# Channel attention on one core: 18 tiles of 64 rows in four slots, and a counted loop on TensorE

## Chip, cores, metric

One core of a Trainium2 chip, the other cores idle. The metric is the device time of one launch in microseconds. Times before and after the change are medians of fast runs; a profile is one run out of them.

## The reference

```
x: (1, 384, 384, 384) bf16, normal * 0.05;  w1d: (1,) bf16
g = mean of x over the 384*384 pixels            # one number for each channel
s = sigmoid(g * w1d[0])
out = x * s                                      # broadcast over the pixels
```

The input is 113.25 MB and so is the output. The mean is needed before the first product is right, and the ring of slots on the chip holds 264 of x's 1152 rows (256 after the change). Both kernels therefore guess: they take the sigmoid of the mean of the first rows, multiply and store with it, sum all rows meanwhile, and compare at the end. In bf16 both sigmoids are the same here, so the second pass, which is in the program for the other case, never runs.

## The kernel before

The 147,456 pixels are 1152 "rows" of 128 partitions. A tile of n rows is one DMA in which each partition moves n x 384 elements that lie on end in device memory. TensorE sums a tile by matmuls with a matrix of ones into three banks, VectorE multiplies it in place, ScalarE's queue stores it. A small planner records operations with what they read and write, and puts in the semaphore waits.

```python
WIDE = 512
EDGE, SLOT, BOTH = 44, 44, 4       # rows of the first tile, of a slot; tiles loaded on two queues
...
    def dram(view, r0, n):
        return view[r0 * P : (r0 + n) * P, :].rearrange("(p t) c -> p (t c)", p=P)
...
    def put(place, n, r0, to):
        plan.op("vector", gate(to, place, n, s_early),
                reads=["s_early"] + rows(place, n), writes=rows(to, n))
        plan.final.append(
            plan.dma("scalar", dram(o_rows, r0, n), at(to, n), reads=rows(to, n)))
...
    for k in range(BOTH):                     # halves of the first tiles on both queues
        load(places[k], sizes[k], starts[k], ("sync", "scalar"))
        if k == 0:
            plan.dma("scalar", w_one[0:1, 0:1], w1d.unsqueeze(0), writes=["w_one"])
    weight()
    add_rows(places[0], sizes[0], 0, True, True)
    add_banks(0, copy=True)
    plan.op("scalar", ...sigmoid -> s_early...)
    for k in range(1, len(sizes)):
        if k >= n_slots:                      # six slots of 44 rows
            j = k - n_slots
            put(places[j], sizes[j], starts[j], places[j])
        if k >= BOTH:
            load(places[k], sizes[k], starts[k])          # sync queue alone
        add_rows(places[k], sizes[k], 1, k == 1, k == last)
    for k in range(len(sizes) - n_slots, last):
        put(places[k], sizes[k], starts[k], places[k])
    put(places[last], sizes[last], starts[last], places[last + 1 - n_slots])
```

Of the kernel before, what the change touches and what calls it, by code (L numbers as in the profile page):

```python
# [13 lines left out]
class Planner:  # L14
# [9 lines left out]
    def __init__(self, nc, name, n_dma_sems):  # L24
        self.nc = nc
        self.streams = {e: [] for e in ("sync", "scalar", "vector", "tensor", "gpsimd")}
        self.sems = {e: nc.alloc_semaphore(f"{name}_{e}") for e in self.COMPUTE}
        self.count = {e: 0 for e in self.COMPUTE}
        self.pool = [nc.alloc_semaphore(f"{name}_dma_{i}") for i in range(n_dma_sems)]
        self.pool_uses = [0] * n_dma_sems  # L30
        self.n_dma = 0
        self.writer = {}
        self.readers = {}
        self.seen = {e: {} for e in self.streams}
        self.final = []

    def _wait(self, engine, token):
        sem, value = token
        if self.seen[engine].get(sem.name, 0) >= value:
            return  # L40
        self.seen[engine][sem.name] = value
        self.streams[engine].append(("wait", sem, value))

    def _needs(self, reads, writes):
        need = {}
        tokens = []
        for r in reads:
            if r in self.writer:
                tokens.append(self.writer[r])
        for r in writes:  # L50
            if r in self.writer:
                tokens.append(self.writer[r])
            tokens.extend(self.readers.get(r, ()))
        for sem, value in tokens:
            if need.get(sem.name, (None, 0))[1] < value:
                need[sem.name] = (sem, value)
        return list(need.values())

    def _record(self, token, reads, writes):
        for r in reads:  # L60
# [5 lines left out]
    def op(self, engine, emit, reads=(), writes=(), signal=True):  # L66


        reads, writes = list(reads), list(writes)
        for token in self._needs(reads, writes):  # L70
            if engine == "tensor" and token[0].name == self.sems["tensor"].name:
                continue
            self._wait(engine, token)
        token = (self.sems[engine], self.count[engine] + 1)
        if signal:
            self.count[engine] += 1
        self.streams[engine].append(("op", emit, self.sems[engine] if signal else None, 1))
        self._record(token, reads, writes)

    def dma(self, engine, out, in_, reads=(), writes=()):  # L80
        reads, writes = list(reads), list(writes)
        for token in self._needs(reads, writes):
            self._wait(engine, token)
        i = self.n_dma % len(self.pool)
        self.n_dma += 1
        if self.pool_uses[i]:
            self._wait(engine, (self.pool[i], 16 * self.pool_uses[i]))
        self.pool_uses[i] += 1
        token = (self.pool[i], 16 * self.pool_uses[i])
        self.streams[engine].append(  # L90
            ("op", lambda e: e.dma_start(out, in_), self.pool[i], 16)  # L91
        )
        self._record(token, reads, writes)
        return token

    def emit(self, name, e):
        for kind, a, b, *c in self.streams[name]:
            if kind == "wait":
                e.wait_ge(a, b)
            else:  # L100
                ins = a(e)
                if b is not None:
                    ins.then_inc(b, c[0])


def split(n, most):
    k = -(-n // most)
    return [n // k + (i < n % k) for i in range(k)]


WIDE = 512
EDGE, SLOT, BOTH = 44, 44, 4


def bass_standalone__channel_attn_eca__vision_kernel(
# [30 lines left out]
    def at(r0, n):  # L146
        assert r0 + n <= n_arena
        return arena[:, r0 * C : (r0 + n) * C]

    def rows(r0, n):  # L150
        return [("sb", r) for r in range(r0, r0 + n)]

    def gate(to, place, n, s):
        s_b = s[:].unsqueeze(1).broadcast_to([P, n, C])
        v, to_v = (at(r, n).rearrange("p (t c) -> p t c", t=n) for r in (place, to))
        return lambda e: e.tensor_tensor(to_v, v, s_b, ALU.mult)  # L156

    n_slots = n_arena // SLOT
    full, rest = divmod(n_rows - EDGE, SLOT)
    if rest < EDGE:  # L160
        full, rest = full - 1, rest + SLOT
    sizes = [EDGE] + [SLOT] * full + [4 * q for q in split(rest // 4, EDGE // 4)]
    assert sum(sizes) == n_rows and max(sizes) <= SLOT
    plan = Planner(nc, "a", 50)

    def load(place, n, r0, queues=("sync",)):
# [26 lines left out]
            )  # L193
        )

    def add_rows(place, n, group, first, last):

        n_wide = n * C // WIDE
        start = place * C
        for i in range(n_wide):  # L200
            bank = acc[group][i % 3]
            plan.op(
                "tensor",
                lambda e, i=i, bank=bank: mm(e,
                    bank[:, :],
                    ones[:],
                    arena[:, start + i * WIDE : start + (i + 1) * WIDE],
                    start=first and i < 3,
                    stop=last and i >= n_wide - 3,
                ),  # L210
                reads=["ones"] + (rows(place, n) if i in (0, n_wide - 1) else []),
                writes=[f"acc{group}"],
                signal=i == n_wide - 1,
            )

    def add_banks(group, copy):

# [10 lines left out]
                )  # L228
            plan.op("vector", emit, reads=[f"acc{group}", "total"], writes=["total"])

    def put(place, n, r0, to):
        plan.op(
            "vector",
            gate(to, place, n, s_early),
            reads=["s_early"] + rows(place, n),
            writes=rows(to, n),
        )
        plan.final.append(
            plan.dma("scalar", dram(o_rows, r0, n), at(to, n), reads=rows(to, n))
        )  # L240

    def weight():

        plan.op(
            "scalar",
            lambda e: e.activation(warm[:, 1:2], warm[:, 0:1], ACT_F.Sigmoid),  # L246
            reads=["warm"],
            writes=["warm1"],
        )
        plan.op(  # L250
            "tensor",
            lambda e: e.matmul(  # L252
                w_all[:, 0:1], ones[0:1, :], w_one[0:1, 0:1], start=True, stop=True
            ),
            reads=["ones", "w_one"],
            writes=["w_all"],
        )
        for i, n in enumerate((sizes[0], n_rows)):
            plan.op(
                "vector",  # L260
                lambda e, i=i, n=n: e.tensor_scalar_mul(  # L261
                    w_scaled[:, i : i + 1], w_all[:, 0:1], 1.0 / float(P * n)
                ),
                reads=["w_all"],
                writes=[f"w_scaled{i}"],
            )

    starts = [sum(sizes[:k]) for k in range(len(sizes))]
    places = [k % n_slots * SLOT for k in range(len(sizes))]
    last = len(sizes) - 1  # L270


    plan.op("gpsimd", lambda e: e.memset(warm[:, 0:1], 0.0), writes=["warm"])  # L273
    plan.op("vector", lambda e: e.memset(ones[:], 1.0), writes=["ones"])  # L274
    for k in range(BOTH):
        load(places[k], sizes[k], starts[k], ("sync", "scalar"))
        if k == 0:
            plan.dma("scalar", w_one[0:1, 0:1], w1d.unsqueeze(0), writes=["w_one"])
    weight()
    add_rows(places[0], sizes[0], 0, True, True)  # L280
    add_banks(0, copy=True)
    plan.op(
        "scalar",
# [3 lines left out]
        reads=["total", "w_scaled0", "warm1"],  # L287
        writes=["s_early"],
    )



    for k in range(1, len(sizes)):
        if k >= n_slots:
            j = k - n_slots
            put(places[j], sizes[j], starts[j], places[j])
        if k >= BOTH:
            load(places[k], sizes[k], starts[k])
        add_rows(places[k], sizes[k], 1, k == 1, k == last)
    for k in range(len(sizes) - n_slots, last):  # L300
        put(places[k], sizes[k], starts[k], places[k])
    put(places[last], sizes[last], starts[last], places[last + 1 - n_slots])


    add_banks(1, copy=False)
# [28 lines left out]
    checked = (plan.sems["vector"], plan.count["vector"])  # L334


    again = Planner(nc, "b", 50)
    for place, n, r0 in zip(places, sizes, starts):
        again.dma("sync", at(place, n), dram(x_rows, r0, n), writes=rows(place, n))
        again.op(  # L340
            "vector",
            gate(place, place, n, s_true),
            reads=rows(place, n),
            writes=rows(place, n),
        )
        again.final.append(
            again.dma("scalar", dram(o_rows, r0, n), at(place, n), reads=rows(place, n))
        )
    for token in again.final:
        again._wait("scalar", token)  # L350
    stored = nc.alloc_semaphore("stored")
# [67 lines left out]
```

## Time and profile before

| | before |
|---|---|
| median, range of 6 runs | 530.79 us, 530.41 to 531.01 |
| span of the profiled run | 528.7 us |
| DMA rate from 100 to 200 us | 433 GB/s |
| data packets, bytes each | 7,424, mostly 33,792 |
| first store issued | 35.6 us |

The page's head says what is busy, the slices when, the windows how much of it in a chosen stretch. Here the DMA row is 9 in all slices but the first and the last, while PE and DVE are each busy for 46% of the span, so the questions are whether the DMA rate is the same everywhere and what the two ends lose. The lines themselves stand in the prediction.

### The profile page before, as it was taken

The page shows a single profiled execution, that of the slowest core. Times are in us where ns is not written, and L with a number is a line of the kernel's source. Part 1 is how long each engine was busy: PE and PEld are TensorE (multiplying, and loading weights), DVE is VectorE, ACT ScalarE, POOL GpSimd, SP SyncE. Part 2 cuts the span into 40 slices and gives each one's busy share as a digit, 9 for nine tenths or more (in the row PEclk, how much of TensorE's full clock was granted, in tenths as well). Part 3 has the DMA queues.
Part 4 walks back from the last instruction along what each step waited for, and adds up shares of the span by engine and source line. Part 5 has one row for each costly group of instructions (what it writes and reads, how often), then busy time and mean ns, then how long its engine had stood idle before and what let it go on. Part 6 is the DMA issues. An engine that isn't in the chain of part 4 may idle for free.

```text
span 528.7 us, 1091 instructions
## 1 busy us (share of the span) xinstructions
PE 245.2 (46%) x865; PEld 0.2 (0%) x2; DVE 241.2 (46%) x45; ACT 2.7 (1%) x4; POOL 0.3 (0%) x5
## 2 busy tenths in 40 slices
PE   0877256165275165174274364264373373365400
PEld 0000000000000000000000000000000000000000
DVE  0299742633624633624624624624615615616720
ACT  1000000000000000000000000000000000000000
POOL 0000000000000000000000000000000000000000
PEclk9989776686676786786875786886875776877665
DMA  8999999999999999999999999999999999999998
GB/s 359 431 427 419 447 429 431 445 414 447 419 442 437 422 447 412 450 428 430 440 419 450 430 429 435 424 450 430 430 431 427 447 429 430 429 443 433 430 420 349
DMA packets 8360, 226.57 MB, mean 429 GB/s; under 512 B 930, under 2 KB 930, under 8 KB 930
## 3 DMA queue, kind: packets, MB, share of 16 engines
q10 hardware_dynamic: 4466, 121.90, 53.5%
q1 hardware_dynamic: 3888, 104.60, 46.1%
q8 instruction: 3, 0.05, 0.0%
q14 instruction: 3, 0.02, 0.0%
HBM read 113.25 MB, written 113.25 MB: 428 GB/s over the span
## 4 chain that ended last, share of the span: by engine, by line
another core or an unknown queue 70%; DMA 16%; DVE 4%; PE 3%; SPq 1%; issue 1%; ACT 0%; ACTq 0%
DMA out_dram<-arena 8%; DMA arena<-in_x_dram 6%; PE acc L184 3%; DVE arena L156 3%; DMA w_one<-in_w1d_dram 2%; SPq L91 1%; DVE total L226 1%; ACT s_true L308 0%; ACT s_early L284 0%; DVE total L316 0%; DVE total L224 0%; DVE wrong L324 0%; PE acc L182 0%; ACTq L91 0%
## 5 line engine op out<-in xcount | busy, mean ns | idle before, releaser
L184 PE MATMUL acc<-arena,ones 128*128 128x512 bf16 x863 | 244.7, 454 | 244.0 <-DMA arena<-in_x_dram 244.0
L156 DVE TENSOR_TENSOR arena<-arena,s_early 128x16896 bf16<-128x16896 bf16 (+2 forms) x27 | 234.5, 8691 | 240.9 <-PE acc L184 237.5
L252 PE MATMUL w_all<-w_one,ones 1*128 1x1 bf16 x1 | 0.2, 159 | 14.1 <-DMA w_one<-in_w1d_dram 14.1
L261 DVE TENSOR_SCALAR w_scaled<-w_all 128x1 f32<-128x1 f32 x2 | 0.2, 152 | 13.3 <-PE w_all L252 13.3
L226 DVE TENSOR_TENSOR total<-total,acc 128x128 f32<-128x128 f32 (+2 forms) x11 | 4.5, 408 | 2.4 <-PE acc L184 2.0
L224 DVE COPY total<-acc 128x384 f32<-128x384 f32 x1 | 0.6, 558 | 8.6 <-PE acc L184 8.6
L308 ACT ACTIVATE s_true<-total,w_scaled 128x384 bf16<-128x384 f32 x1 | 0.6, 614 | 479.5 <-DVE total L226 479.5
L246 ACT ACT_TABLE_LOAD x1 | 1.3, 1283 | 3.4 <-issue 3.4
L316 DVE TENSOR_TENSOR total<-s_true,s_early 128x384 f32<-128x384 uint16 x1 | 0.6, 559 | 0.7 <-ACT s_true L308 0.7
L284 ACT ACTIVATE s_early<-total,w_scaled 128x384 bf16<-128x384 f32 x1 | 0.6, 614 | 21.1 <-DVE total L226 21.1
L182 PE MATMUL acc<-arena,ones 128*128 128x512 bf16 x1 | 0.6, 590 | 0.0
L324 DVE TENSOR_REDUCE wrong<-total 128x1 f32<-128x384 f32 x1 | 0.6, 553 | 0.0
L274 DVE MEMSET ones<- 128x128 bf16 x1 | 0.2, 165 | 0.8 <-PEq L404 0.8
L246 ACT ACTIVATE warm<-warm 128x1 f32<-128x1 f32 x1 | 0.2, 203 | 0.0
L330 DVE CAST redo<-wrong 128x1 int32<-128x1 f32 x1 | 0.2, 154 | 0.0
L182 PEld LDWEIGHTS acc<-arena,ones 128*128 128x128 bf16 x1 | 0.1, 105 | 0.0
L252 PEld LDWEIGHTS w_all<-w_one,ones 1*128 1x128 bf16 x1 | 0.1, 99 | 14.1 <-issue 14.1
L404 POOL MEMSET const-bfloat16-1.0<- 128x1 bf16 x1 | 0.1, 102 | 0.0
L404 POOL MEMSET const-uint8-127<- 128x1 uint8 x1 | 0.1, 102 | 0.0
L273 POOL MEMSET warm<- 128x1 f32 x1 | 0.1, 99 | 0.3 <-POOLq L404 0.3
L404 POOL MEMSET const-float32-0.0<- 128x1 f32 x1 | 0.1, 99 | 0.2 <-issue 0.2
L404 POOL MEMSET const-float32-1.0<- 128x1 f32 x1 | 0.1, 99 | 0.0
## 6 DMA issues: line engine op xcount, KB each, us to landing
out_dram<-arena ACTq DMA_DIRECT2D x25, 4224.0 KB, 62.3
arena<-in_x_dram SPq DMA_DIRECT2D x21, 4224.0 KB, 38.7
arena<-in_x_dram ACTq DMA_DIRECT2D x4, 2112.0 KB, 27.2
arena<-in_x_dram SPq DMA_DIRECT2D x4, 2112.0 KB, 26.9
arena<-in_x_dram SPq DMA_DIRECT2D x1, 2688.0 KB, 35.1
out_dram<-arena ACTq DMA_DIRECT2D x1, 2688.0 KB, 29.2
arena<-in_x_dram SPq DMA_DIRECT2D x1, 2304.0 KB
out_dram<-arena ACTq DMA_DIRECT2D x1, 2304.0 KB, 26.9
```

The lines of the kernel that those rows point to most:

```text
L91: ("op", lambda e: e.dma_start(out, in_), self.pool[i], 16)
L156: return lambda e: e.tensor_tensor(to_v, v, s_b, ALU.mult)
L182: loaded.append(e.matmul(bank, weights, moving, start=start, stop=stop))
L184: return e.add_instruction(mybir.InstMatmult(name=nc.get_next_instruction_name(), engine=mybir.EngineType.PE, ins=[e.lower_ap(moving), e.l ...
L224: emit = lambda e, part=part, of=of: e.tensor_copy(part, of)
L226: emit = lambda e, part=part, of=of: e.tensor_tensor(part, part, of, ALU.add)
L246: lambda e: e.activation(warm[:, 1:2], warm[:, 0:1], ACT_F.Sigmoid),
L284: lambda e: e.activation(s_early[:], total[:], ACT_F.Sigmoid, scale=w_scaled[:, 0:1]),
L308: lambda e: e.activation(s_true[:], total[:], ACT_F.Sigmoid, scale=w_scaled[:, 1:2]),
L316: lambda e: e.tensor_tensor(total[:], s_true[:].bitcast(U16), s_early[:].bitcast(U16), ALU.not_equal),
L324: lambda e: e.reduce_max(wrong[:], total[:], axis=mybir.AxisListType.X),
L404: nc = _bacc.Bacc("TRN2", target_bir_lowering=False, num_devices=1)
```

## The change

It makes larger tiles (18 of 64 rows, four slots), sums and multiplies them in units of 32 rows, so that VectorE may start before TensorE has summed the whole tile, and folds most of TensorE's program into a counted loop: GpSimd waits for each load and raises a count, TensorE waits for the count. The planner also drops waits that another wait implies. Two things come along with the tile size: only the first **two** tiles are loaded on both queues now, and the last tile is multiplied in place.

```diff
-EDGE, SLOT, BOTH = 44, 44, 4
+UNIT, TILE, BOTH = 32, 64, 2
...
+    def add_unit(e, group, column, start, stop):
+        for i in range(n_wide):
+            last = mm(e, acc[group][i % 3][:, :], ones[:],
+                arena[:, bass.ds(column + i * WIDE, WIDE)],
+                start and i < 3, stop and i >= n_wide - 3)
+        return last
...
+    def sum_others():
+        def one(e, column, stop):
+            e.wait_ge(ready, 1).then_inc(ready, -1)
+            add_unit(e, 1, column, False, stop).then_inc(plan.sems["tensor"], 1)
+        def emit(e):
+            with e.Fori(2, n_units - 1) as u:
+                one(e, e.snap((u & (ring - 1)) * (UNIT * C)), False)
+            one(e, (n_units - 1) % ring * UNIT * C, True)
...
-    def put(place, n, r0, to):
+    def put(k):
+        place, r0 = k % n_slots * TILE, k * TILE
+        for u in range(k * per_tile, (k + 1) * per_tile):
+            plan.op("vector", gate(...unit u...), reads=["s_early"] + unit(u), writes=unit(u))
         plan.final.append(plan.dma("scalar", ...whole tile...))
...
     for k in range(BOTH):
-        load(places[k], sizes[k], starts[k], ("sync", "scalar"))
+        load(k * TILE, TILE, k * TILE, ("sync", "scalar"))
...
-        add_rows(places[k], sizes[k], 1, k == 1, k == last)
+        for u in range(k * per_tile, (k + 1) * per_tile):
+            plan.relay(ready, "gpsimd", "tensor", reads=unit(u), writes=["acc1"])
```

Not printed here: the planner's clocks, by which it knows what a wait implies, and the second pass, which doesn't run.

More of the change, by code (lines that the diff above doesn't have):

```diff
@@ L34, in __init__, with _clock @@
         self.seen = {e: {} for e in self.streams}
+        self.clocks = {}
         self.final = []
+    def _clock(self, engine, token):
+        known = dict(self.seen[engine])
+        known[token[0].name] = max(known.get(token[0].name, 0), token[1])
+        self.clocks[token[0].name, token[1]] = known
     def _wait(self, engine, token):
         sem, value = token
-        if self.seen[engine].get(sem.name, 0) >= value:
+        seen = self.seen[engine]
+        if seen.get(sem.name, 0) >= value:
             return
-        self.seen[engine][sem.name] = value
+        for name, at in self.clocks[sem.name, value].items():
+            seen[name] = max(seen.get(name, 0), at)
         self.streams[engine].append(("wait", sem, value))
@@ L56, in _needs @@
                 need[sem.name] = (sem, value)
-        return list(need.values())
+        return [
+            (sem, value)
+            for sem, value in need.values()
+            if not any(
+                self.clocks[s.name, v].get(sem.name, 0) >= value
+                for s, v in need.values()
+                if s.name != sem.name
+            )
+        ]
     def _record(self, token, reads, writes):
@@ L77, in op @@
         self.streams[engine].append(("op", emit, self.sems[engine] if signal else None, 1))
+        self._clock(engine, token)
         self._record(token, reads, writes)
@@ L92, in dma, with relay @@
         )
+        self._clock(engine, token)
         self._record(token, reads, writes)
         return token
+    def relay(self, sem, via, to, reads, writes):
+        for token in self._needs(reads, []):
+            self._wait(via, token)
+        self.streams[via].append(("op", lambda e: e.sem_inc(sem, 1), None, 0))
+        for name, at in self.seen[via].items():
+            self.seen[to][name] = max(self.seen[to].get(name, 0), at)
+        self.count[to] += 1
+        token = (self.sems[to], self.count[to])
+        self._clock(to, token)
+        self._record(token, reads, writes)
     def emit(self, name, e):
@@ L99, in emit @@
                 e.wait_ge(a, b)
+            elif kind == "block":
+                a(e)
             else:
@@ L151, in rows, with unit @@
         return [("sb", r) for r in range(r0, r0 + n)]
+    def unit(u):
+        return rows(u % ring * UNIT, UNIT)
     def gate(to, place, n, s):
@@ L156, in gate @@
         return lambda e: e.tensor_tensor(to_v, v, s_b, ALU.mult)
-    n_slots = n_arena // SLOT
-    full, rest = divmod(n_rows - EDGE, SLOT)
-    if rest < EDGE:
-        full, rest = full - 1, rest + SLOT
-    sizes = [EDGE] + [SLOT] * full + [4 * q for q in split(rest // 4, EDGE // 4)]
-    assert sum(sizes) == n_rows and max(sizes) <= SLOT
+    n_slots = n_arena // TILE
+    n_units, per_tile = n_rows // UNIT, TILE // UNIT
+    n_tiles, ring = n_rows // TILE, n_slots * per_tile
+    assert n_rows % TILE == 0 and TILE % UNIT == 0 and UNIT * C % (3 * WIDE) == 0
+    assert ring & (ring - 1) == 0
+    n_wide = UNIT * C // WIDE
+    ready = nc.alloc_semaphore("ready")
     plan = Planner(nc, "a", 50)
@@ L194, in mm, with sum_unit @@
         )
-    def add_rows(place, n, group, first, last):
-        n_wide = n * C // WIDE
-        start = place * C
+    def add_unit(e, group, column, start, stop):
         for i in range(n_wide):
-            bank = acc[group][i % 3]
-            plan.op(
-                "tensor",
-                lambda e, i=i, bank=bank: mm(e,
-                    bank[:, :],
-                    ones[:],
-                    arena[:, start + i * WIDE : start + (i + 1) * WIDE],
-                    start=first and i < 3,
-                    stop=last and i >= n_wide - 3,
-                ),
-                reads=["ones"] + (rows(place, n) if i in (0, n_wide - 1) else []),
-                writes=[f"acc{group}"],
-                signal=i == n_wide - 1,
-            )
+            last = mm(
+                e,
+                acc[group][i % 3][:, :],
+                ones[:],
+                arena[:, bass.ds(column + i * WIDE, WIDE)],
+                start and i < 3,
+                stop and i >= n_wide - 3,
+            )
+        return last
+    def sum_unit(u):
+        plan.op(
+            "tensor",
+            lambda e: add_unit(e, u, u * UNIT * C, True, u == 0),
+            reads=["ones"] + unit(u),
+            writes=[f"acc{u}"],
+        )
+    def sum_others():
[6 more added lines that the diff above has]
+            one(e, (n_units - 1) % ring * UNIT * C, True)
+        plan.streams["tensor"].append(("block", emit, None))
     def add_banks(group, copy):
@@ L229, in add_banks @@
             plan.op("vector", emit, reads=[f"acc{group}", "total"], writes=["total"])
-    def put(place, n, r0, to):
-        plan.op(
-            "vector",
-            gate(to, place, n, s_early),
-            reads=["s_early"] + rows(place, n),
-            writes=rows(to, n),
-        )
+    def put(k):
+        place, r0 = k % n_slots * TILE, k * TILE
+        for u in range(k * per_tile, (k + 1) * per_tile):
+            plan.op(
+                "vector",
+                gate(u % ring * UNIT, u % ring * UNIT, UNIT, s_early),
+                reads=["s_early"] + unit(u),
+                writes=unit(u),
+            )
         plan.final.append(
-            plan.dma("scalar", dram(o_rows, r0, n), at(to, n), reads=rows(to, n))
+            plan.dma(
+                "scalar", dram(o_rows, r0, TILE), at(place, TILE), reads=rows(place, TILE)
+            )
         )
@@ L257, in weight @@
         )
-        for i, n in enumerate((sizes[0], n_rows)):
+        for i, n in enumerate((UNIT, n_rows)):
             plan.op(
@@ L266, in weight @@
             )
-    starts = [sum(sizes[:k]) for k in range(len(sizes))]
-    places = [k % n_slots * SLOT for k in range(len(sizes))]
-    last = len(sizes) - 1
     plan.op("gpsimd", lambda e: e.memset(warm[:, 0:1], 0.0), writes=["warm"])
@@ L279, in bass_standalone__channel_attn_eca__vision_kernel @@
     weight()
-    add_rows(places[0], sizes[0], 0, True, True)
+    sum_unit(0)
     add_banks(0, copy=True)
@@ L289, in bass_standalone__channel_attn_eca__vision_kernel @@
     )
-    for k in range(1, len(sizes)):
+    sum_unit(1)
+    sum_others()
+    for k in range(1, n_tiles):
         if k >= n_slots:
-            j = k - n_slots
-            put(places[j], sizes[j], starts[j], places[j])
+            put(k - n_slots)
         if k >= BOTH:
-            load(places[k], sizes[k], starts[k])
-        add_rows(places[k], sizes[k], 1, k == 1, k == last)
-    for k in range(len(sizes) - n_slots, last):
-        put(places[k], sizes[k], starts[k], places[k])
-    put(places[last], sizes[last], starts[last], places[last + 1 - n_slots])
+            load(k % n_slots * TILE, TILE, k * TILE)
+        for u in range(k * per_tile, (k + 1) * per_tile):
+            plan.relay(ready, "gpsimd", "tensor", reads=unit(u), writes=["acc1"])
+    for k in range(n_tiles - n_slots, n_tiles):
+        put(k)
     add_banks(1, copy=False)
@@ L334, in bass_standalone__channel_attn_eca__vision_kernel @@
     checked = (plan.sems["vector"], plan.count["vector"])
-    again = Planner(nc, "b", 50)
-    for place, n, r0 in zip(places, sizes, starts):
+    again = Planner(nc, "b", 30)
+    half, r0 = n_arena // 2, 0
+    for k, n in enumerate(split(n_rows, half)):
+        place = k % 2 * half
         again.dma("sync", at(place, n), dram(x_rows, r0, n), writes=rows(place, n))
@@ L348, in bass_standalone__channel_attn_eca__vision_kernel @@
         )
+        r0 += n
     for token in again.final:
```

## The prediction

> **What bounds the kernel now.** I read the page's head and slices first, then the windows (busy time by stretch), then the chain of waits, then the groups by line, then the DMA issues.
>
> ```profile
> span 528.7 us, 1091 instructions
> PE 245.2 (46%) x865; PEld 0.2 (0%) x2; DVE 241.2 (46%) x45; ACT 2.7 (1%) x4; POOL 0.3 (0%) x5
> DMA  8999999999999999999999999999999999999998
> DMA packets 8360, 226.57 MB, mean 429 GB/s; under 512 B 930, under 2 KB 930, under 8 KB 930
> ```
>
> No compute engine is busy for half of the span, and the DMA row is full from the second slice to the last but one. The bytes are the input read once and the output written once, which the change does not touch. The windows (start:end, length, busy time of PE, PEld, DVE, ACT, POOL, clock, DMA share, GB/s) say where the rate is not full:
>
> ```profile
> 0.00:2.00 2.00, 0.00 (x0) 0.00 (x0) 0.17 (x1) 0.00 (x0) 0.30 (x5) 1.00 0.51 110
> 2.00:4.00 2.00, 0.00 (x0) 0.00 (x0) 0.00 (x0) 0.63 (x1) 0.00 (x0) 1.00 0.73 287
> ...
> 100.00:200.00 100.00, 47.29 (x165) 0.00 (x0) 44.74 (x6) 0.00 (x0) 0.00 (x0) 0.72 1.00 433
> ...
> 524.00:526.00 2.00, 0.00 (x0) 0.00 (x0) 0.00 (x0) 0.00 (x0) 0.00 (x0) 0.50 0.88 378
> 526.00:528.00 2.00, 0.00 (x0) 0.00 (x0) 0.00 (x0) 0.00 (x0) 0.00 (x0) 0.50 0.20 83
> ```
>
> In between it is 433 GB/s. At that rate 226.57 MB take 523.3 us. The start loses (433-110)x2 + (433-287)x2 = 938 KB, which is 2.2 us. The end, from 524 to 528.7, moves 0.92 MB where 2.04 would fit, 2.6 us lost. 523.3 + 2.2 + 2.6 = 528.1 of the 528.7 in the span. So the kernel is bound by the DMA engines all the way, and only two ends of some 2 us and the 433 itself could be better. The metric is 1.9 us above the span (530.6 against 528.7); I take that as fixed.
>
> The waits agree: each compute engine waits for the one before it, and the first waits for loads.
>
> ```profile
> PE acc L184 <- DMA arena<-in_x_dram: 244.0, 26, 11.3
> DVE arena L156 <- PE acc L184: 237.5, 23, 11.9
> ```
>
> The DMA issues give the depth of the queues: KB each and us from issue to landing.
>
> ```profile
> out_dram<-arena ACTq DMA_DIRECT2D x25, 4224.0 KB, 62.3
> arena<-in_x_dram SPq DMA_DIRECT2D x21, 4224.0 KB, 38.7
> ```
>
> A 44-row tile is 4.325 MB; in and out, 8.65 MB at 433 GB/s, it takes 20.0 us. So a load spends two periods in its queue and a store three. With some 18.6 us for the sum (9 to 10) and the multiply (8.96), a slot's cycle is 119.6 us, which is the six slots times 20.0. Both queues always hold more than one transfer: that is why the DMA never stops.
>
> [...] loads and stores both have the 20.0 us period. [...] the trace has 58 full DMAs, 58x16 + 2 = 930, exactly its packets under 512 B. [...] the trace has 33 matmuls in 7.28 us when warm (221 ns each) and in 8.7 to 10.2 us after an idle stretch.
>
> **The change part by part.**
>
> *Tiles.* 27 tiles of up to 44 rows become 18 of 64, six slots become four (264 rows of ring become 256). Bytes are unchanged. DMAs go from 59 to 39: 38 full ones of 144 packets, so about 5,480 packets in place of 8,360, of 49,152 B a row in place of 33,792. [...] I take 0.5.
>
> *Start.* The first half tile is now 32 rows and shares the DMA with the other half: 6.29 MB/433 + 2.2 = 16.7 us; the weight landed 1.6 us after the first half before, so 18.3. Then 24 matmuls with a cold start (33 took 8.9, less nine warm ones) 7.0, the banks' six additions 2.75, the sigmoid 0.7: 28.8 us, against 26.6. The multiply by shapes took 8,958 ns for 16,896 elements and 4,959 for 9,216: 0.521 ns an element, so 6.56 us for 12,288. Two of them: the first store at 42.0 us, where it was 35.6. That costs nothing, as four tiles of loads, 25.2 MB, keep the queue full until 60 us even alone.
>
> *Steady state.* The period is 12.58 MB/433 = 29.1 us. TensorE needs 48 matmuls: 10.6 warm, plus 1.4 to 2.9 for the slow start, 12.0 to 13.5 us; VectorE 13.1, one unit behind it. From landing to store it is about 13 + 6.6 + 0.5 = 20 us of a period of 29. When the first store begins to move (about 43.6 us with 1.5 for the issue, an estimate), loads are ahead by (43.6-2.2)x433 = 17.9 MB, 2.85 tiles, and with even shares that lead stays. Of the four slots 0.7 are being worked on, so about two tiles are waiting as stores and one as a load. The load queue is the thinner: store j ends when loads have moved j + 3.85 tiles, so load j+4 may come 0.15 period, 4.4 us, before the queue is empty, about 3 of which go on landing and issue. If it does run dry for a moment, stores take the whole rate: no byte is lost. So the deeper or shallower ring is worth zero.
>
> *End.* At the last load's last byte 17.9 MB of stores are left; the last one, 14.5 us long, must be ready when the 11.6 MB before it are gone, 26.8 us later. It needs about 1.3 to land, 20 to be summed and multiplied, 1.5 to be issued: 22.8. Four us of slack; before, the last tile was small and was written to another slot so as not to wait for the sum. The end loss stays 2.6 us, unless TensorE is slower.
>
> *The loop.* The listing of the built program shows the body as 24 pairs of one register instruction and one matmul, and a branch; TensorE's listed instructions fall from 867 to 127. The page shows 0.05 + 0.02 MB of instruction transfers in all, so the shorter program saves under 0.2 us of DMA time. A unit may take up to 29.1/2 = 14.5 us, 606 ns a matmul against 221, before TensorE is the bound. GpSimd is idle (0.3 us busy)[...]. The dropped waits are ones already met; zero.
>
> Sum: 530.6 - 0.5 (packets) - 0.1 (instruction transfers) + 0.3 (my allowance for a hole at the end) = 530.3 us.
>
> **The rivals.**
> 1. *The loop makes TensorE slow.* Against it: the margin of 606 ns a matmul. For it: no trace here shows a matmul with an address in a register. At 500 ns, a unit in the loop takes 12 us. Only one of the last tile's two units is in the loop, so its sum takes 17 to 19 us in place of 13, and the end is longer by 0 to 2 us: 530 to 533. At 1 us a matmul TensorE would be the bound: 17 tiles of 48 us, over 800. I hold that at about 2%.
> 2. *Four slots are too few.* If landing, issue and work took 10 us longer than I count, one queue would empty at times, but for a hole both must. The end is where it would show first: each us over the slack of four is a us of the time. A hole of 2 to 4 us makes 532 to 534.
> 3. *Longer rows move at another rate.* [...] Or rows 48 KiB apart, with every tile 6 MiB from the next, meet in the memory more than rows 33 KiB apart: 1% less would be 536. The trace shows mixed, load-only and store-only stretches (427 to 433)[...].
> 4. *The wrong-guess path.* If the sigmoid of the first 32 rows differed from that of all, the second pass would about double the time. Both are 0.5 in bf16 for such inputs, with 32 rows as with 44; under 1%.
>
> **Range and chances.** A gain over 2% means 520 us[...]: 1%. A loss over 2% needs rival 1 or 3 in strong form: 4%. The rest is within 2%. The range, 527.8 to 534[...].
>
> **What would show it.** DMA share 9 in all inner slices and 432 to 435 GB/s in the windows; about 5,480 packets, 610 under 512 B; loads landing about 35 to 40 us and stores about 55 to 60 after issue; the multiply at 6.56 us x36; the first store at about 42 us; a tail after the last byte like before. A slice with DMA at 7 or less near the end would mean the last tile's work stuck out; matmuls far over 0.3 us in the loop, rival 1; inner windows under 430, rival 3. I should be wrong if the queues are not shared evenly, or if a register address costs TensorE more than twice a matmul.

## The result and the profile after

| | before | after |
|---|---|---|
| median, range of 6 runs | 530.79, 530.41 to 531.01 | 537.34, 534.67 to 541.09 |
| span of the profiled run | 528.7 | 533.1 |

The ratio of the fast runs is 1.0124 (95% interval 1.0084 to 1.0164). A ratio here is the mean time of one kernel's fast runs over that of the other's of the same rounds, so it isn't quite the ratio of the medians. By the 2% rule that is "same", but it is clear of the noise, and it lies outside the range. The scatter is new, too: 6.4 us where the kernel before has 0.6.

The head of the page after, with the slices' DMA rows and the packet count:

```profile
span 533.1 us, 2009 instructions
PE 223.1 (42%) x865; PEld 0.2 (0%) x2; DVE 241.0 (45%) x54; ACT 2.7 (1%) x4; POOL 0.3 (0%) x5
DMA  8999999999999999999999999999999999999997
GB/s 356 435 444 417 373 402 384 424 439 439 424 439 439 420 443 435 420 446 432 428 443 432 424 446 424 443 435 424 443 435 420 446 432 420 450 428 428 439 428 318
DMA packets 5475, 226.50 MB, mean 425 GB/s; under 512 B 610, under 2 KB 610, under 8 KB 610
```

The DMA row is as full as before. The row beneath it is the one that tells: from the fifth to the seventh slice (53 to 93 us) the engines are busy and move 373 to 402 GB/s. **Busy is not the same as fast.** The windows of the kernel after (start:end, length, busy time of PE, PEld, DVE, ACT, POOL, clock, DMA share, GB/s):

```profile
40.00:60.00 20.00, 13.83 (x56) 0.00 (x0) 18.58 (x4) 0.00 (x0) 0.00 (x0) 0.83 1.01 398
60.00:80.00 20.00, 2.81 (x13) 0.00 (x0) 10.69 (x2) 0.00 (x0) 0.00 (x0) 0.70 1.00 396
80.00:100.00 20.00, 12.39 (x48) 0.00 (x0) 11.52 (x2) 0.00 (x0) 0.00 (x0) 0.84 0.99 398
100.00:200.00 100.00, 37.82 (x144) 0.00 (x0) 40.58 (x7) 0.00 (x0) 0.00 (x0) 0.67 1.00 434
```

and the same stretches of the kernel before:

```profile
40.00:60.00 20.00, 10.57 (x49) 0.00 (x0) 19.28 (x3) 0.00 (x0) 0.00 (x0) 0.96 1.02 433
60.00:80.00 20.00, 9.74 (x33) 0.00 (x0) 9.33 (x2) 0.00 (x0) 0.00 (x0) 0.67 1.00 433
80.00:100.00 20.00, 10.00 (x33) 0.00 (x0) 8.74 (x2) 0.00 (x0) 0.00 (x0) 0.67 1.00 432
```

At a DMA share of 0.99 to 1.02 in both, 60 us at 397 in place of 433 GB/s lose (433-397) x 60/433 = 5.0 us, and the span is longer by 4.4. From 100 to 200 us the two kernels move bytes equally fast (434 and 433 GB/s). So the whole loss is in the first fifth of the run, and it begins where the first store does. The timeline of ScalarE's queue after:

```profile
29.63 0.61 ACT L335 ACTIVATE s_early<-total,w_scaled 128x384 bf16<-128x384 f32 x1 [26.01 <-DVE total L278]
43.34 0.36 ACTq L109 DMA_DIRECT2D out_dram<-arena  x1
```

The trace also records every DMA packet with its queue, start, duration and size. In the quiet part a 49,152-byte packet takes 1.82 us. I counted, over 38 to 110 us, the packets more than a tenth over that: 115 of them, up to 3.7 us long, loads and stores alike. Their excess, divided by 16 engines, is **4.8 us**. That count is used below for every run.

What the loop and the tail did, from the timeline at the end of the kernel after:

```profile
494.77 12.13 PE L221 MATMUL acc<-arena,ones 128*128 x48 [16.04 <-PEq L258]
501.75 13.03 DVE L192 TENSOR_TENSOR arena<-arena,s_early 128x12288 bf16<-128x12288 bf16 x2 [15.13 <-PE acc L221]
514.70 2.69 DVE L278 TENSOR_TENSOR total<-total,acc 128x384 f32<-128x384 f32 x6
514.82 0.34 ACTq L109 DMA_DIRECT2D out_dram<-arena  x1
```

The last tile was summed in 12.1 us and its store issued 20.1 us after TensorE began on it; the store ahead of it landed at 517.9, so the queue never ran dry. Neither the loop nor the end explains the loss.

### The profile page after: what moved, and what is told of

It is laid out like the page before. It is cut to its first block, busy times and chain, and to the rows that moved or that the text cites. A ratio compares the mean times of both kernels' runs of the same rounds, so it can differ in the third digit from the quotient of the medians.

```text
span 533.1 us, 2009 instructions
## 1 busy us (share of the span) xinstructions
PE 223.1 (42%) x865; PEld 0.2 (0%) x2; DVE 241.0 (45%) x54; ACT 2.7 (1%) x4; POOL 0.3 (0%) x5
## 2 busy tenths in 40 slices
DMA packets 5475, 226.50 MB, mean 425 GB/s; under 512 B 610, under 2 KB 610, under 8 KB 610
## 3 DMA queue, kind: packets, MB, share of 16 engines
q1 hardware_dynamic: 2592, 106.96, 47.1%
## 5 line engine op out<-in xcount | busy, mean ns | idle before, releaser
L192 DVE TENSOR_TENSOR arena<-arena,s_early 128x12288 bf16<-128x12288 bf16 x36 | 234.4, 6555 | 250.8 <-PE acc L221 250.1
L221 PE MATMUL acc<-arena,ones 128*128 (+1 forms) x863 | 222.6, 425 | 264.4 <-PEq L258 264.4
L219 PE MATMUL acc<-arena,ones 128*128 128x512 bf16 x1 | 0.6, 608 | 0.0
## 6 DMA issues: line engine op xcount, KB each, us to landing
out_dram<-arena ACTq DMA_DIRECT2D x18, 6144.0 KB, 56.3
arena<-in_x_dram SPq DMA_DIRECT2D x16, 6144.0 KB, 38.5
```

Source lines behind the costliest of these rows:

```text
L192: return lambda e: e.tensor_tensor(to_v, v, s_b, ALU.mult)
L219: loaded.append(e.matmul(bank, weights, moving, start=start, stop=stop))
L221: return e.add_instruction(mybir.InstMatmult(name=nc.get_next_instruction_name(), engine=mybir.EngineType.PE, ins=[e.lower_ap(moving), e.l ...
```

## The experiments

The matmuls that take their address from a register couldn't be run again in experiments, so the base of nearly all of them is u1, the changed kernel with the loop written out. Kernels of one batch share a chip and the runs of the kernel before. "First store" is the start of the first data packet of a store, "fourth load" that of the fourth tile's load; they and the excess come from the one profiled run of each.

### u1: the loop written out

```diff
-                arena[:, bass.ds(column + i * WIDE, WIDE)],
+                arena[:, column + i * WIDE : column + (i + 1) * WIDE],
...
-    def sum_others(): ...Fori, counts by GpSimd...
+    def sum_later(u):
+        plan.op("tensor",
+            lambda e: add_unit(e, 1, u % ring * UNIT * C, False, u == n_units - 1),
+            reads=["ones"] + unit(u), writes=["acc1"])
```

> The changed kernel with TensorE's loop written out and no counts by GpSimd: tiles of 64, units of 32, first two tiles on both load queues. Theory T (tiles or start make the DMA slow between 40 and 100 us): as the changed kernel, 534 to 541 us, scattered, with 40 to 100 us under 410 GB/s. Rival L (the loop, its registers and counts do it): 530 to 531.5, steady, with 430 or more there.

536.18 us (533.64 to 540.27), ratio 1.0120 (1.0085 to 1.0155): all of the loss, and the scatter, without loop, registers or GpSimd. Its windows:

```profile
40.00:60.00 20.00, 15.46 (x64) 0.00 (x0) 20.00 (x4) 0.00 (x0) 0.00 (x0) 0.91 1.00 393
60.00:80.00 20.00, 0.42 (x2) 0.00 (x0) 10.00 (x2) 0.00 (x0) 0.00 (x0) 0.57 0.99 374
80.00:100.00 20.00, 12.25 (x47) 0.00 (x0) 9.96 (x2) 0.00 (x0) 0.00 (x0) 0.83 1.00 406
```

The same slow stretch. The loop is out as the cause: 48 matmuls take 12.0 to 13.1 us here in the steady state, and 12.1 to 13.0 in the loop.

### u2, u3, u4: tile size and start queues, each alone

u2 is u1 with one number changed, u3 and u4 are the kernel before with one or two:

```diff
 u2 -UNIT, TILE, BOTH = 32, 64, 2
    +UNIT, TILE, BOTH = 32, 64, 4
 u3 -EDGE, SLOT, BOTH = 44, 44, 4
    +EDGE, SLOT, BOTH = 64, 64, 4
 u4 -EDGE, SLOT, BOTH = 44, 44, 4
    +EDGE, SLOT, BOTH = 44, 44, 2
```

> As u1_unrolled, but the first four tiles are loaded on both queues, as the kernel before does. Theory S (stores that begin while only the sync queue still loads cause the slow stretch): 530 to 532 us and 430 GB/s from 40 to 100 us. Theory P (the 48 KiB rows do it): 534 or more, as u1.

531.30 us (530.49 to 533.61, the highest being the profiled run), ratio 1.0013 (1.0000 to 1.0026).

> The kernel before with tiles of 64 rows in four slots and nothing else: whole tiles, first four on both queues. Theory P (48 KiB rows): 534 or more, slow stretch. Theory S (queues at the start): 530 to 532.

530.79 us (530.20 to 534.60, one of six above 531.1, and that one is the profiled run), ratio 1.0002 (0.9989 to 1.0015).

> The kernel before (44 rows, six slots) with only the first two tiles on both load queues. Theory S: 533 to 540 us, with a stretch under 415 GB/s after the first store. Theory P: 530 to 531.

531.06 us (530.67 to 535.76, one of six above 531.3), ratio 1.0023 (0.9996 to 1.0051).

Neither the 64-row tiles nor the two-tile start costs it alone; u1, which has both, loses it (v4 below shows that these two aren't enough either). That went against both theories as I had put them. With four tiles on both queues, the stores stand behind loads on ScalarE's queue, and the first store's data starts only at 61 us, when the loads are nearly through. u2's windows show no long slow stretch (the 423 is that of half-size load packets just before the first store comes, 0.6 us of excess):

```profile
40.00:60.00 20.00, 15.60 (x63) 0.00 (x0) 20.00 (x4) 0.00 (x0) 0.00 (x0) 0.91 1.01 423
60.00:80.00 20.00, 11.77 (x47) 0.00 (x0) 20.00 (x4) 0.00 (x0) 0.00 (x0) 0.90 1.02 441
80.00:100.00 20.00, 0.00 (x0) 0.00 (x0) 2.74 (x1) 0.00 (x0) 0.00 (x0) 0.50 1.00 435
```

### v1, v2, v4: addresses, and the units

In the slow runs the fourth load and the first store go through their tiles side by side: after the change they land at 80.8 and 81.0 us. Do they meet in device memory (v1: other spacing there) or in the on-chip memory (v2: slots two rows further apart)? v4 asks if the 32-row units matter.

```diff
 v1 -        return view[r0 * P : (r0 + n) * P, :].rearrange("(p t) c -> p (t c)", p=P)
    +        return view.rearrange("(p t) c -> p (t c)", p=P)[:, r0 * C : (r0 + n) * C]
 v2 +    def place_of(u):
    +        u %= ring
    +        return u // per_tile * (TILE + 2) + u % per_tile * UNIT
 v4 (before) EDGE, SLOT, BOTH = 64, 64, 2
```

> u1_unrolled with other addresses in device memory: a partition owns 1152 rows on end, so rows of a tile are 864 KiB apart from partition to partition and two tiles 48 KiB apart, with the same packets, tiles, slots and order. Theory H (load and store meet at like addresses in the device memory): 530 to 532, no slow stretch. Theories B (on-chip memory) and J (a store stream that joins a running load stream upsets the engines, whatever the addresses): 534 to 540, as u1.

534.90 us (533.38 to 537.40), ratio 1.0091 (1.0068 to 1.0114): still slow, perhaps a little less.

> u1_unrolled with the slots 66 rows apart in the on-chip memory in place of 64, so slots no longer start 48 KiB apart. Theory B (load and store meet in the on-chip memory): 530 to 532. Theories H and J: 534 to 540, as u1.

537.21 us (535.17 to 540.34), ratio 1.0121 (1.0093 to 1.0149): no help at all.

> The kernel before with 64-row slots and only the first two tiles on both load queues; whole tiles are multiplied, the last into a free slot. If tile size and start queues together are enough: 534 to 540, as u1. If the 32-row units matter too: 530 to 532, as u3_before64.

530.86 us (530.22 to 532.77), ratio 1.0002 (0.9989 to 1.0015). Not slow, with the same tiles and start queues as u1. What differs in its start: whole tiles are summed and multiplied, so the first store is issued at 48.9 us and not at 44.2.

### v3, w1, w2: the first store moved back

v3 holds the first store until one more unit is multiplied; w1 and w2 put three and six idle activations ahead of it on ScalarE.

```diff
 v3 -        for u in range(k * per_tile, (k + 1) * per_tile):
    +        for u in {0: (0, 1, 2), 1: (3,)}.get(k, (2 * k, 2 * k + 1)):
    ...
    -                ... reads=rows(place, TILE)
    +                ... reads=rows(place, TILE) + (unit(2) if k == 0 else [])
 w1 +        if k == 0:
    +            for _ in range(3):        # w2: 6
    +                plan.op("scalar", lambda e: e.activation(s_true[:], total[:], ...),
    +                    reads=["total", "w_scaled0"] + unit(1), writes=["s_true"])
```

> u1_unrolled with the first store held until one more unit is multiplied, 6.6 us later, so that it begins about a third of a tile behind the fourth load and not together with it. Theory F (the two streams go through a tile in step): 530 to 533, slow stretch gone. Theory J (joining a running load stream): 534 to 540, as u1.

530.80 us (530.39 to 532.05), ratio 1.0006 (0.9993 to 1.0019). The loss is gone, and most of the scatter with it, by **holding one DMA back** for six microseconds. Its queue of stores and its windows (the first is still low, by (433-413) x 20/433 = 0.9 us: 19 load packets that begin from 51.9 to 56.0 us are long as the store joins, and they do not come back):

```profile
50.45 461.28 ACTq L109 DMA_DIRECT2D out_dram<-arena  x18
```

```profile
40.00:60.00 20.00, 15.84 (x65) 0.00 (x0) 20.00 (x4) 0.00 (x0) 0.00 (x0) 0.91 1.00 413
60.00:80.00 20.00, 8.24 (x28) 0.00 (x0) 10.67 (x3) 0.00 (x0) 0.00 (x0) 0.66 1.01 438
80.00:100.00 20.00, 4.30 (x20) 0.00 (x0) 12.18 (x2) 0.00 (x0) 0.00 (x0) 0.66 1.00 433
```

> u1_unrolled with three idle activations on ScalarE ahead of the first store, some 2 us: the first store is issued at about 45.5 to 46 us in place of 43.5, and its data starts as the fourth load starts (about 47). Theory F (slow if the store starts with or just ahead of the fourth load, in step): still slow, 533 or more. Theory G (slow only if the store starts while the third load has a few packets left): 530 to 532.

537.15 us (531.38 to 542.04); the two slowest runs are left out of the ratio, 1.0087 (1.0054 to 1.0121). Still slow. The activations held the issue less than I had reckoned: it came at 44.7 us, while they ran from 43.4 to 45.3. The first packet came at 48.9, as in u1, so w1 is u1 once more and doesn't tell the theories apart.

> As w1_delay3 with six idle activations, some 4 us: issue at about 48 us, data about a packet behind the start of the fourth load, as in v4_before64_both2. Theories F and G both: 530 to 532. If slow: the start time of the first store is not the cause.

532.44 us (530.26 to 533.17), ratio 1.0029 (1.0013 to 1.0045), first packet at 49.9: most of the loss is gone, though both theories had expected all of it to go.

### y2: the first store moved forward

If an early first store were bad by itself, an earlier one should be worse. y2 loads the first tile by quarters and the weight first.

```diff
+    plan.dma("scalar", w_one[0:1, 0:1], w1d.unsqueeze(0), writes=["w_one"])
...
+            for i in range(0, TILE, 16):
+                plan.dma(("sync", "scalar")[i // 16 % 2], at(i, 16),
+                    of[:, i * C : (i + 16) * C], writes=rows(i, 16))
```

> u1_unrolled with the first unit loaded by quarters on both queues and the weight first, so that the first store comes some 6 to 8 us earlier, about 36 us, well inside the third load in place of at its end. Theory F (only a start that leaves the store in step with the fourth load is slow): 530 to 532.5. Theory E (the earlier the store joins the lone load queue, the worse): 537 or more.

530.69 us (530.08 to 531.82, 13 runs), ratio 1.0005 (0.9996 to 1.0013). Not slow. The first packet came at 43.4 us, some 9 us ahead of the fourth load, which now starts at 52.5.

### z1: the fourth load moved instead

All runs so far moved the store. z1 leaves it and holds the fourth load until the third unit is multiplied.

```diff
+        if k == 3:
+            put(0)
...
+            load(k % n_slots * TILE, TILE, k * TILE, after=unit(2) if k == 3 else ())
```

> u1_unrolled with the first store issued as in u1 (about 43.5 us) and the fourth load held until the third unit is multiplied, so its first packet comes about 52 us, 5 to 6 us after the store's first packet, where u1 has the two 1 to 3 us apart. The first store moves alone meanwhile, so no byte is lost. Theory F (in step is what costs): 530 to 531.5, few packets over 1.82 us. If the time of the first store alone matters: 534 to 540.

533.00 us (529.95 to 541.89, 22 runs), ratio 1.0048 (1.0029 to 1.0066). Ten of the 22 runs lie under 532, the others go up to 537 and once to 542 (that one is left out of the ratio). The store's first packet came at 46.3, the load's at 53.9, and the three windows show 423, 425 and 424 GB/s. So parting the two from the load's side takes away 0.7 of the 1.2 per cent, and not all as I had expected. What z1 keeps of u1 is that the store's first packets come just when the third load ends (its last packet starts at 45.2).

### w3: the same start with 44-row tiles

u4 with five idle activations ahead of the first store, as in w1.

> u4_before_both2 (44-row tiles, two tiles on both queues, first store issued at 35.9) with five idle activations, some 3.3 us, so that the first store comes about 2 us ahead of the end of a load, as in the changed kernel. If the start phase alone is the cause, whatever the row length: 534 or more. If it takes the 48 KiB rows as well: 530 to 532.

532.12 us (530.36 to 535.23), ratio 1.0023 (1.0008 to 1.0039). The first store's packet (43.1 us) came half a microsecond after the fifth load's (42.6). Some runs are slow, but the loss is a fifth of u1's. The kernel before, too, has its fifth load start at 42.0 and its first store at 44.3, side by side, and no run of it is slow; there loads stand on both queues until then: the store was issued at 35.6 us, and the last load ahead of it on ScalarE's queue ended at 43.9.

### w4, y3: without compute

Both give a wrong result on purpose. w4 multiplies one row in 32 and fills in the time with 21 idle activations; y3 does so with 17 and also does three matmuls of 24 from the third unit on.

```diff
-                gate(u % ring * UNIT, u % ring * UNIT, UNIT, s_early),
+                gate(u % ring * UNIT, u % ring * UNIT, 1, s_early),
 y3 +        n_wide = 3 if few else UNIT * C // WIDE
```

> Wrong result on purpose: u1_unrolled with one row of each unit multiplied in place of 32, so VectorE is nearly idle, and 21 idle activations that put the first store back to about 43 to 45 us. Theory V (VectorE's traffic in the on-chip memory slows the transfers from 40 to 100 us): 530 to 532. If the DMA queues alone do it: 533 to 540, and packets over 1.82 us from 44 us on, as u1.

534.62 us (530.35 to 536.41), ratio 1.0071 (1.0039 to 1.0104). The store came too late for a clean test (first packet 49.9, as in w2), yet four of six runs took 533 or more. The profiled run is one of the two that didn't.

> Wrong result on purpose: as w4_no_multiply, with 17 idle activations, so the first store is issued near 43.5 us as in u1, and with 3 of 24 matmuls in each unit from the third on, so TensorE and VectorE hardly read the on-chip memory. If the DMA queues alone do it: 534 to 540 as u1. If compute traffic is needed: 530 to 532.

534.86 us (533.57 to 536.29), ratio 1.0075 (1.0061 to 1.0089), first packet at 46.9. So compute isn't needed for a loss. Whether it has a part in its size isn't shown: the excess fell from 5.5 us (u1) to 1.2, but y3's store also came 0.7 us ahead of the fourth load where u1's came 2.7 us behind it, and w4, with as little multiplying, lost more than w2 (ratios 1.0071 and 1.0029) at what its one profile shows to be the same first packet. That 1.2 us of mean excess made 4 us of time is seen in y3's windows at its end:

```profile
40.00:60.00 20.00, 2.72 (x6) 0.00 (x0) 0.72 (x2) 2.72 (x5) 0.00 (x0) 0.59 1.01 415
...
524.00:526.00 2.00, 0.00 (x0) 0.00 (x0) 0.00 (x0) 0.00 (x0) 0.00 (x0) 0.50 0.51 221
526.00:528.00 2.00, 0.00 (x0) 0.00 (x0) 0.00 (x0) 0.00 (x0) 0.00 (x0) 0.50 0.06 25
528.00:530.00 2.00, 0.00 (x0) 0.00 (x0) 0.00 (x0) 0.00 (x0) 0.00 (x0) 0.50 0.06 25
530.00:532.00 2.00, 0.00 (x0) 0.00 (x0) 0.00 (x0) 0.00 (x0) 0.00 (x0) 0.50 0.11 49
```

With 16 engines in the share, 0.06 is one engine's worth (0.11 at most two engines'), still at work for some 6 us after the rest. When it fell behind is seen in the semaphore increments, which the trace has too: 16 for a DMA, as many as there are engines. (That each comes from an engine of its own is my reading; the trace names no engines.) In y3 the last of them came 1.2 us after the median for the third load (49 us), 6.2 for the first store (75 us), 9.5 for the second (98 us) and 7.8 for the last. In w3's profiled run, the slowest of its six, it was 0.2 us at 45 us, 7.6 at 102 and 6.2 at the end. (In the kernel before it is 1.5 at the end, in v3 1.4.) So most of the lag of the first 100 us was still there at the end. That the engine had no idle time in which to catch up is my estimate, from the DMA share of 1.00 in all of y3's windows from 60 to 500 us. The mean rate of a stretch hides such a lag (433 and 430 GB/s from 60 to 100 us), and so does the excess (1.2 us).

### y4: shifted reads

Wrong on purpose: loads read 17 pixels (12.75 KiB) further on, stores don't, so like places of a load and a store no longer have like addresses.

```diff
-        of = dram(x_rows, r0, n)
+        of = x_rows[r0 * P + 17 : (r0 + n) * P + 17, :].rearrange(...)     # not for the last tile
```

> Wrong result on purpose: u1_unrolled with loads that read 17 rows (12.75 KiB) further on, so that load and store in step no longer have like addresses within the device memory. Theory H: 530 to 532. Otherwise as u1, 534 to 540.

536.09 us (535.46 to 537.89), ratio 1.0114 (1.0099 to 1.0130). With v1 this leaves nothing for addresses in device memory as a main cause.

### y1: stores on the sync queue

```diff
-                "scalar", dram(o_rows, r0, TILE), at(place, TILE), reads=rows(place, TILE)
+                "sync", dram(o_rows, r0, TILE), at(place, TILE), reads=rows(place, TILE)
```

> u1_unrolled with the stores on the sync queue, between the loads, so no two transfers alternate on an engine: a store's data starts when the loads ahead of it are through, about 62 us. Theory A (the slow stretch is two queues sharing the engines): 530 to 531, all packets at the single-queue time. It is also the candidate for a version as good as the kernel before. If 534 or more: sharing isn't needed.

534.66 us (533.81 to 534.89), ratio 1.0070 (1.0056 to 1.0084). A miss. There is no long slow stretch (430, 424, 433 GB/s in the three windows), and one queue carries all loads and stores after the start. On one queue a DMA follows the one ahead of it: in the kernel before, loads on the sync queue start at 21.8, 31.9 and 42.0 us, and those ahead of them end at 22.2, 32.3 and 42.4. Yet, as in y3, part of the engines' work is late: from 526 to 532 us the windows show 123, 98 and 49 GB/s at DMA shares of 0.28, 0.23 and 0.11. Unlike in y3 the lag grows little by little: the last increment came 1.0 us after the median at 62 us, 2.5 at 76, 4.5 at 294 and 6.3 at the end. It isn't a version to take.

### Together

| run | first store, first packet | fourth load, first packet | excess, us | profiled run, us | median, us |
|---|---|---|---|---|---|
| y2 | 43.4 | 52.5 | 0.8 | 530.54 | 530.69 |
| z1 | 46.3 | 53.9 | 0.9 | 532.90 | 533.00 |
| v1 | 46.8 | 46.1 | 3.8 | 535.10 | 534.90 |
| y3 (no compute) | 46.9 | 47.6 | 1.2 | 536.29 | 534.86 |
| after | 47.1 | 46.1 | 4.8 | 534.67 | 537.34 |
| y4 | 47.1 | 46.0 | 4.6 | 535.46 | 536.09 |
| v2 | 48.0 | 46.0 | 5.1 | 539.33 | 537.21 |
| u1 | 48.8 | 46.1 | 5.5 | 536.45 | 536.18 |
| w2 | 49.9 | 46.0 | 0.9 | 531.90 | 532.44 |
| v4 | 52.9 | 46.1 | 0.8 | 532.77 | 530.86 |
| v3 | 54.2 | 46.1 | 0.8 | 530.92 | 530.80 |
| u2 | 61.3 | (on both queues) | 0.0 (0.6 with half-size packets) | 533.61 | 531.30 |

(w1's profile fell in a run that was left out of its ratio, at 2.6 us of excess, and w4's in one of its quick runs; both are left out here.) With compute as it is, there is one band: a first packet 0.7 to 2.7 us after the fourth load's, which is also 1.5 to 3.3 us after the third load's last packet has started, gives 3.8 to 5.5 us of excess. A first packet 3.9 us or more after the fourth load's, or 7.6 us or more ahead of it, gives under one. Each row rests on one profiled run, and the excess isn't all that a run can lose: u2's and v4's profiled runs have little of it and still took 533.61 and 532.77 us. In v4's the last increment of the last store came 4.2 us after the median.

No experiment beat the kernel before. The best with 64-row tiles (u3, v3, y2, v4) are level with it, at medians of 530.69 to 530.86 us against 530.79.

## Why the prediction was wrong

**What held.** The bound, and nearly every step about it: 5,475 packets (5,480 predicted), 610 small ones (610), a multiply of 6,555 ns (6.56 us), 12.1 to 13.0 us for 48 matmuls (12.0 to 13.5), loads landing after 38.5 us and stores after 56.3 (35 to 40, 55 to 60), 434 GB/s in the steady state, the first store issued at 43.3 us (42.0; the weight landed a microsecond later), though its first packet came 3.7 us after that and not 1.5. That 1.5 was an estimate: in the trace before, the first load's first packet came 1.0 us after its issue began. So was the 1.3 us for the last load to land; its last packet ended at 492.2 and its last increment came at 494.4. The last store was issued at 514.8 and the one before it landed at 517.9: 3.1 us of slack where I had about four. The loop is harmless, as u1 shows by being as slow without it. The 0.5 us taken for fewer packets and the low end of the range, 527.8 us, were my estimates, and no trace here shows them; the rate from 100 to 200 us was 434 GB/s with 49,152-byte packets and 433 with 33,792. One piece of evidence was weak: loads and stores have the same period because every slot is loaded and stored once in a cycle, and that says nothing of how an engine goes from one queue to the other. The packets say more: if each is matched with the one that ends as it starts (an estimate, for the trace names no engines), about nine in ten of an engine's successive packets change the queue from 100 to 450 us of the kernel before.

**What failed** is a step that I treated as settled: "That costs nothing, as four tiles of loads, 25.2 MB, keep the queue full until 60 us even alone." The queue was full, but a full queue was taken to mean 433 GB/s at any time, and from 40 to 100 us it moved 396 to 398. The term is missing from the sum. Its size in the profiled run was 4.8 us by the packets' excess: 530.3 + 4.8 = 535.1, where that run took 534.67. The other five runs had more, up to 541; they aren't profiled.

**Rival 3** had the sign that I named for it, inner windows under 430, but for 60 us only and not for its reason. Longer rows do 434 GB/s in the steady state, and u3 and v4 run 64-row tiles at the old time. The spacing of addresses, a guess that no trace had shown, isn't it (ratios of 1.0091, 1.0121 and 1.0114 in v1, v2 and y4). Rivals 1 and 4 didn't happen. Of rival 2 only the harmless half did: after the change the load queue stood empty from 78.6 to 84.5 us, but in v3 it did so for longer, from 69.3 to 82.9, at 438 and 433 GB/s in its windows; an empty load queue cost nothing there while stores stood in theirs, as predicted.

**What is shown.** The loss depends on when the first store joins the loads. Moving that one DMA later (v3, 530.80 us), earlier (y2, 530.69) or behind loads on its own queue (u2, 531.30), where u1 took 536.18, takes away all or nearly all of it; v3 holds back nothing else, y2 and u2 change the loads of the start too. The rest of the setting matters as well: the two-tile start (u2) leaves the sync queue loading alone when the store comes (after the change, ScalarE's last load ends at 33.4 us and the store's first packet comes at 47.1), and the units of 32 rows make the store come just then (v4 has it 4 us later). That it takes the large tiles is shown only in part: u4's first store (40.8 us) came 7.5 us or more from the start of any load, and w3, which put it beside one, lost a fifth. Once the first store and the fourth load go side by side they land together (80.8 and 81.0 us after the change). Why packets are slow again from 82 to 92 us (307 GB/s from 86 to 90) isn't shown: the second store (78.0 us) and the fifth load (84.5) start no closer together than in v3 (75.9 and 82.9), which has no such stretch. From then on the landings are some 9.5 us apart, and slow packets are over.

**What stays open** is what makes packets up to twice as long there (3.7 us in place of 1.82). It may be that the two streams begin together, or that the store's first packets meet the end of a load: in the band above both are true, and z1, which parts them, got rid of only part of the loss. It isn't any two streams side by side: the kernel before runs so from 44 us on, at 432 to 434 GB/s in its windows to 480. Whether compute traffic makes it larger is open too (y3 and w4 point different ways). Nor does this account cover y1, where one queue carries everything after the start and the lag grew little by little (1.0 us at 62 us, 6.3 at the end), or w4, whose slow runs weren't profiled.

## What to carry to other kernels

In this kernel, which the DMA engines bound all the way, "the queue is never empty" wasn't enough: the DMA share stayed at 0.99 to 1.01 while the rate was 397 GB/s in place of 433. So look at GB/s in such a kernel, and not only at the busy share, in each stretch, above all where a second stream joins the first. When it gets slower and scatters more with the same bytes (here a range of 6.4 us in place of 0.6), try moving the first transfer of the second stream by a few microseconds before you doubt the engines' programs; here one extra wait was worth the whole loss (u1 536.18 us, v3 530.80). In y3 and w3 most of a lag from the first 100 us was still there at the end (7.8 us of 9.5, 6.2 of 7.6), so look at the last few microseconds as well: one or two engines' worth of work there, 25 to 49 GB/s for some 6 us in y3, is a loss that the mean rates ahead of it, 430 and 433 GB/s, didn't show.
